# Fox attention with a bilinear feed-forward network: decay vectors spread over the partitions by GpSimd instead of by copying transfers

## The chip, the cores and the metric

The kernel runs on one core of a Trainium2 chip. The core has four engines that compute (TensorE, here PE with its weight loads as PEld; VectorE, DVE; ScalarE, ACT; GpSimd, POOL), a fifth, SyncE (SP), that mostly issues transfers, and 16 DMA engines. Each engine runs its own list of instructions in order and waits at semaphores for the others. The metric is the device time of one execution in microseconds (us); lower is better.

## What is computed

For 8 batches of 8 heads with 576 positions and head size 64, the reference forms attention scores with a decay, takes a causal softmax, and puts the result through a bilinear feed-forward network (d_model 512, d_ff 1536) on 4608 tokens:

```python
scores = scale * np.matmul(q, k.transpose(0, 1, 3, 2))
log_f = np.log(np.clip(f, 0.0001, 1.0))
cum = np.cumsum(log_f, axis=-1)
decay = cum[:, :, :, None] - cum[:, :, None, :]
scores = np.where(causal, -1000000000.0, scores + decay)
...
attn = attn / (np.sum(attn, axis=-1, keepdims=True) + 1e-09)
return np.matmul(attn, v)
...
x = attn_out.transpose(0, 2, 1, 3).reshape(B * S, H * D)
a = x @ w_a
b = x @ w_b
return a * b @ w_out
```

The part of the decay that varies along a row of scores is one vector of 576 numbers per head, the decay vector (`cum` of that head). In a tile of scores the 128 partitions are query positions, so each partition needs the same vector.

## The kernel before

Heads are worked in pairs: `t` from 0 to 31 is a pair, four pairs a batch, and two pairs (four heads, `u`) share their score matmuls. For each pair the kernel computes score tiles by 128 query rows (PE, line 390), then a row maximum, an exponential with its row sum (ACT, lines 537 and 543), a reciprocal (DVE, 550 and 552), a scaling by it (GpSimd, line 560, f16 in place), transposes of the probabilities (DMA transposes on SP's queue, line 576), the product with `v` (PE, lines 604 to 629) and a copy into `xT`. Once the tokens of a block are complete, the feed-forward network runs over them (PE, lines 877 and 897), with its copies and products on ACT and DVE and its stores on SP's queue (line 907). Matmuls of the network fill PE while the attention of later batches is on the other engines. After the last pair only the network's last blocks are left.

The first two batches (`DIRECT` = 2, pairs 0 to 7) add the decay with extra matmuls. The other 24 pairs take it from a tile `spread`: four buffers (`spread_79` to `spread_82`), each with the vectors of both heads of a pair on all 128 partitions. The cumulative sums are stored once in DRAM as `cum_d` (64 x 576). `load_spread` (line 451) reads two rows of it with one DMA that copies them to 128 partitions, 576 KB written. Then GpSimd makes masked copies (`mask_copy` 458, `mask_tail` 464, later `mask_last` 469), and DVE adds vector and scores and takes the maximum in one instruction (`do_decay`, line 508). A `spread` buffer is free for the pair four later once the last of these has read it.

GpSimd also casts q, k and v to f16 (lines 139 and 141).

The kernel is written as a list of small operations, and the table `ORDER` fixes the one sequence in which all of them are emitted; each engine's list is that sequence cut down to its own operations. `CHOICE` fixes the engine for those that can run on several. Nothing is reordered when it runs.

Of the kernel before, what the change touches and what calls it, by code (L numbers as in the profile page):

```python
# [9 lines left out]
FP32 = mybir.dt.float32  # L10
# [27 lines left out]
def kernel(  # L38
# [11 lines left out]
    nc = tc.nc  # L50
# [12 lines left out]
    def pool(name, bufs=1, **kw):  # L63
        return ctx.enter_context(tc.tile_pool(name=name, bufs=bufs, **kw))
# [7 lines left out]
    T = {}  # L72
# [27 lines left out]
    RING = {"S": 2, "bc": 4, "n32": 3, "n16": 2, "PA": 3, "PB": 2, "PTA": 2, "PTB": 2, "st": 6, "ht": 14, "a16": 3, "osb": 2, "ff": 4}  # L100
# [17 lines left out]
    osb_pool = pool("osb", RING["osb"])  # L118
    ps = pool("ps", 1, space=bass.MemoryType.PSUM)
# [177 lines left out]
    def batch_inputs(b):  # L297
# [4 lines left out]
        for which, part, gm in items:  # L302
# [18 lines left out]
            ld = op("S", "ldqk", lambda _, which=which, hh=hh: load_qk(b, which, hh))  # L321
# [13 lines left out]
            tp = op("D", "tqk", lambda _, which=which, hh=hh: transpose_qk(b, which, hh), cas)  # L335
# [304 lines left out]

    last_row = [[] for _ in range(RING["bc"])]
    ev_ops, late, last_pb = {}, {}, [[] for _ in range(RING["PB"])]

    def decay_rows(t):
# [17 lines left out]
        ld = op("S", "ldb", lambda _: load_spread(t), [o6])  # L662
# [306 lines left out]
    for n in [256, 256, 256, 384] + [512] * 6 + [384]:  # L969
# [13 lines left out]
        215 81 216 202 203 276 204 7 201 180 207 208 281 285 181-183 1641 90 1642 441 187 317 289 188 189  # L983
        318 290 166 323 324 295 297 296 190 1645 1643 1644 319 325 217 218 1646 1647 165 1648 88 229 192 231
        459 291 221 223 191 230 257 224 258 209 232 255 222 279 184 256 280 286 235-237 444 238 329 205 186
# [5 lines left out]
        1682-1684 1680 316 364 340 249 1685 283 251 443 379 252 376 20 250 1687 404 380 1688 1691 398 381  # L991
        449 344 407 546 1689 1690 409 452 382 408 1693 372 1692 1695-1697 365 1694 347 348 371 464 349 357
# [6 lines left out]
        523 483 1737 1740-1742 492 493 488 489 509 494 524 510 477 516 539 525 526 1738 527 470 451 462 497  # L999
        498 1743 495 466 428-430 499 431 547 484 437 439 438 440 490 530 531 500 457 491 537 501 1745 1746  # L1000
# [4 lines left out]
        553 551 606 636 566 573 1791 574 557 558 575 576 607-609 653 1790 1793 1794 1792 637 559 578 577 579  # L1005
        555 610 611 580 552 1795 1798 1799 650 615-617 582-584 581 1796 560 639 548 612 642 556 620 622 627
        654 600 544 614 618 1800 1803 1804 1807 621 585 613 587 619 629 623 624 586 626 1805 625 630 1801
        588-590 1806 591 593 592 628 1808 1811 657 1809 1813 1810 1812 669 1815 1817 702 703 739 704 651
        1816 643 1814 709 670 705 1819 1820 638 710 655 1818 711 1823 676 1821 1825 671 1822 640 712-714
# [4 lines left out]
        688 696 698 744 728 699 726 1857 1858 735 730 1854 1855 641 694 700 729 731 732 701 747 1861-1863  # L1014
# [5 lines left out]
        788-790 818 825 820 791 826 848 819 1892 821-823 1893-1895 855 900 1896 867 908 868 824 907 828 902  # L1020
# [3 lines left out]
        862 906 920 883 921 885 1916-1918 938 1919 886 1920 1921 888 889 922 923 1922 839 850 866 887 1924  # L1024
        893 894 935 942 890 895 854 926 844 891 896 892 927-929 897 924 933 1032 898 1923 1925 1926 1929 945
# [103 lines left out]
```

## Time and profile before

| | us |
|---|---|
| three runs, median (lowest to highest) | 405.43 (403.7 to 407.23) |
| the profiled execution: time | 402.69 |
| the profiled execution: span on the core | 400.9 |
| TensorE's mean granted clock | 0.985 |
| transfers of `spread` | 24 of 576 KB, median 5.9 from issue to landing |
| bytes moved in all | 80.71 MB, 201 GB/s over the span |

A profile row gives a source line, an engine, an operation and the tiles that it writes and reads, then a count, the busy time and the mean of one in nanoseconds, and the idle time of the engine just before such instructions with what ended it. Between the span and the device time lie 402.69 - 400.9 = 1.8 us that no row shows.

### The profile page before, as it was taken

To read this page: it belongs to the slowest core of one execution; us is meant where nothing else is said; L and a number is where in the kernel's file an instruction comes from. 1 tells how busy PE (TensorE), PEld (TensorE's weight loads), DVE (VectorE), ACT (ScalarE), POOL (GpSimd) and SP (SyncE) were. 2 spreads that over 40 slices of the span, in tenths; PEclk is the share of its full clock that TensorE was granted. 3 is DMA by queue.
4 is the path that set the end of the run, shared out by engine and by line. 5 is a ranking of instruction groups with operands and counts; after the bars stand their busy time and mean duration, and the time that the engine had idled before them with its cause. 6 is when DMAs were issued, how large, how long until landed. Compare 5 with 4: busy or idle time off the path is not lost.

```text
span 400.9 us, 10798 instructions
## 1 busy us (share of the span) xinstructions
PE 378.9 (95%) x3856; PEld 209.3 (52%) x3856; DVE 315.5 (79%) x958; ACT 250.6 (63%) x756; POOL 262.8 (66%) x438
## 2 busy tenths in 40 slices
PE   5679799989999999999999999999999999999996
PEld 5557575765846544444545454544454444444553
DVE  5879997979998988989899789899959893373450
ACT  2678895768768777758785777675868673310111
POOL 4988899787967796979696948697858753000000
PEclk9869999999999999999999999999999999999999
DMA  7999999999999999999899998999997827101102
GB/s 245 261 217 224 253 284 224 233 209 225 208 281 224 267 199 305 202 310 191 270 217 286 238 301 168 242 242 243 255 199 192 151 68 177 54 0 53 55 2 78
DMA packets 149466, 80.71 MB, mean 201 GB/s; under 512 B 130660, under 2 KB 133476, under 8 KB 149412
## 3 DMA queue, kind: packets, MB, share of 16 engines
q1 hardware_dynamic: 145492, 75.02, 79.1%
q0 software_dynamic: 3696, 4.72, 7.0%
q8 instruction: 30, 0.49, 0.5%
q10 hardware_dynamic: 224, 0.28, 0.2%
q14 instruction: 24, 0.20, 0.1%
HBM read 52.20 MB, written 9.58 MB: 154 GB/s over the span
## 4 chain that ended last, share of the span: by engine, by line
PE 69%; DMA 8%; DVE 8%; POOL 5%; ACT 4%; issue 4%; SPq 0%; POOLq 0%; ACTq 0%; DVEq 0%
PE psb L877 20%; PE psa L877 20%; PE pso L897 16%; PE sc L390 7%; DVE st L484 3%; PE pv L604 2%; DMA PTB<-PB 2%; POOL PA L560 2%; DMA spread<-cum_d 2%; DMA k<-in_k_dram 2%; PE idle L174 1%; DVE ht L888 1%; DVE S L508 1%; DMA out_dram<-osb 1%; DMA xT<-PA 1%
## 5 line engine op out<-in xcount | busy, mean ns | idle before, releaser
L877 PE MATMUL psb<-xT,wb 128*128 128x512 f16 (+2 forms) x528 | 115.2, 341 | 2.4 <-DVE a L141 1.3
L877 PE MATMUL psa<-xT,wa 128*128 128x512 f16 (+2 forms) x528 | 115.2, 341 | 0.5 <-ACT osb L137 0.2
L508 DVE CUSTOM_DVE_ANT_0 S<-sc,spread 128x128 f32<-128x128 f32 (+3 forms) x192 | 104.3, 567 | 7.8 <-PE sc L390 6.7
L560 POOL TENSOR_SCALAR PA<-PA,st 128x128 f16<-128x128 f16 (+2 forms) x180 | 84.4, 482 | 33.8 <-DVE st L552 19.8
L897 PE MATMUL pso<-wout,ht 128*128 128x512 f16 (+1 forms) x444 | 98.4, 374 | 0.0
L888 DVE TENSOR_TENSOR ht<-psb,a 128x512 f16<-128x512 f32 (+2 forms) x132 | 76.7, 588 | 14.1 <-PE psb L877 10.1
L543 ACT ACTIVATE PA<-S,st 128x256 f16<-128x256 f32 (+2 forms) x144 | 71.9, 501 | 22.9 <-DVE st L508 21.4
L877 PEld LDWEIGHTS <-wb 128*128 128x128 f16 x528 | 49.8, 98 | 45.7 <-issue 6.8
L877 PEld LDWEIGHTS <-wa 128*128 128x128 f16 x528 | 50.4, 98 | 42.7 <-issue 2.0
L560 POOL TENSOR_SCALAR PB<-PB,st 128x512 f16<-128x512 f16 (+1 forms) x90 | 62.8, 712 | 10.6 <-DVE st L552 5.9
L897 PEld LDWEIGHTS <-ht 128*128 128x128 f16 x444 | 41.8, 98 | 48.1 <-issue 2.8
L137 ACT CAST a<-psa 128x512 f16<-128x512 f32 (+2 forms) x85 | 42.7, 511 | 34.8 <-PE psa L877 33.4
L390 PE MATMUL sc<-kT,qT 32*128 32x128 f16 (+5 forms) x960 | 41.3, 272 | 6.8 <-DVE qT L294 4.6
L543 ACT ACTIVATE PB<-S,st 128x512 f16<-128x512 f32 x48 | 34.3, 716 | 8.1 <-DVE st L508 7.4
L484 DVE TENSOR_REDUCE st<-sc 128x1 f32<-128x576 f32 (+8 forms) x48 | 31.4, 693 | 6.8 <-PE sc L390 5.2
L141 DVE CAST a<-psa 128x512 f16<-128x512 f32 (+2 forms) x47 | 26.2, 558 | 11.3 <-PE psa L877 10.8
L390 PEld LDWEIGHTS <-qT 32*128 32x128 f16 (+1 forms) x960 | 19.0, 96 | 28.8 <-issue 12.3
L552 DVE RECIPROCAL st<-st 128x2 f32<-128x2 f32 x128 | 18.6, 157 | 11.5 <-ACT PB L543 6.1
L537 ACT ACTIVATE PB<-S,st 128x576 f16<-128x576 f32 x24 | 18.6, 775 | 13.9 <-DVE st L508 5.0
L543 ACT ACTIVATION_READ_ACCUMULATOR PA<-S,st 128x1 f32 x144 | 27.2, 189 | 0.0
L137 ACT COPY osb<-pso 128x512 f32<-128x512 f32 (+1 forms) x26 | 14.4, 563 | 20.3 <-PE pso L897 18.6
L141 POOL CAST k<-k 128x1152 f16<-128x1152 f32 (+2 forms) x16 | 22.1, 1384 | 5.0 <-DMA k<-in_k_dram 5.0
(87 smaller groups left out, 449.8 us busy)
## 6 DMA issues: line engine op xcount, KB each, us to landing
spread<-cum_d SPq DMA_DIRECT2D x24, 576.0 KB, 5.9
out_dram<-osb SPq DMA_DIRECT2D x35, 256.0 KB, 4.0
k<-in_k_dram SPq DMA_DIRECT2D x15, 576.0 KB, 6.5
q<-in_q_dram SPq DMA_DIRECT2D x15, 576.0 KB, 6.9
v<-in_v_dram SPq DMA_DIRECT2D x32, 256.0 KB, 6.7
wout<-in_moe_w_out_dram POOLq DMA_DIRECT2D x3, 512.0 KB, 11.0
wa<-in_moe_w_a_dram POOLq DMA_DIRECT2D x1, 1024.0 KB, 13.9
v<-in_v_dram SPq DMA_DIRECT2D x8, 128.0 KB, 6.0
```

What stands on the lines that cost most here:

```text
L137: nc.scalar.copy(out=out_, in_=in_)
L141: ENG[e].tensor_copy(out=out_, in_=in_)
L390: nc.tensor.matmul(out=dst, lhsT=lhsT, rhs=rhs, start=start, stop=stop, skip_group_check=True)
L484: nc.vector.tensor_reduce(out=m if i == 4 else st[:, 2 * i:2 * i + 2][:, h:h + 1] if isinstance(x, list) else m, in_=y, axis=AXX, op=MAX, ...
L508: nc.vector.tensor_tensor_reduce(out=o, in0=x, in1=y, scale=-1.0, scalar=3e38, op0=ADD, op1=MIN, accum_out=m)
L537: nc.scalar.activation(out=p_blocks(t, 4), in_=T[("s" if direct else "z", t, 4)], func=EXP, bias=st[:, 8:9], scale=sign, accum_out=st[:, 1 ...
L543: nc.scalar.activation(out=p_blocks(t, i)[:, :, h, :], in_=x.rearrange("p (j k) -> p j k", k=128), func=EXP, scale=sign, bias=st[:, c:c + ...
L552: nc.vector.reciprocal(out=st[:, 20 + 2 * i:22 + 2 * i], in_=st[:, 10 + 2 * i:12 + 2 * i])
L560: ENG[e].tensor_scalar(out=p, in0=p, scalar1=st[:, c:c + 1], scalar2=1.0, op0=MUL, op1=MUL)
L877: nc.tensor.matmul(out=p[:, 0:n], lhsT=w16[:, db, 128 * fb:128 * fb + 128], rhs=xTflat[db][:, t0:t0 + n], start=(db == 0), stop=(db == 3))
L888: nc.vector.tensor_tensor(out=ht[:, 0:n], in0=T.pop(("psb", t0, fb))[:, 0:n], in1=T.pop(("a16", t0, fb))[:, 0:n], op=MUL)
L897: nc.tensor.matmul(out=o, lhsT=T[("ht", t0, fb)][:, 128 * tb:128 * tb + 128], rhs=wout16[:, fb, c], start=(fb == 0), stop=(fb == 11))
```

## The change

The DMA that wrote two heads' vectors onto 128 partitions is gone. For four heads (`u`), one load brings four rows of `cum_d`, 9 KB, into a new tile `rw`, on partitions 0, 32, 64 and 96. For each pair, two GpSimd instructions (`partition_broadcast`) each copy one of these rows to all 128 partitions of `spread`. There are 12 loads and 48 broadcasts. `rw` has one buffer, and the ring `ht` (products of the network) has 13 buffers instead of 14. The masked copies are as before. `ORDER` and `CHOICE` are new throughout.

```diff
-    RING = {... "st": 6, "ht": 14, "a16": 3, "osb": 2, "ff": 4}
+    RING = {... "st": 6, "ht": 13, "a16": 3, "osb": 2, "ff": 4, "rw": 1}
...
-    def load_spread(t):
-        nc.sync.dma_start(out=spread[t % RING["bc"]][:, :, SM:SM + S],
-                          in_=cum_d.rearrange("(n h) s -> n (h s)", h=2)[t:t + 1, :].to_broadcast(
-                              [128, 2 * S]).rearrange("p (h s) -> p h s", h=2))
+    def load_rows(u):
+        x = T[("rw", u)] = rw_pool.tile([128, S], FP32, tag="rw", name="rw")
+        nc.sync.dma_start(out=x.rearrange("(h r) s -> h r s", r=32)[:, 0, :], in_=cum_d[4 * u:4 * u + 4, :])
+
+    def spread_rows(t):
+        for h in range(2):
+            nc.gpsimd.partition_broadcast(spread[t % RING["bc"]][:, h, SM:SM + S], T[("rw", t // 2)][RG[2 * (t % 2) + h], :])
...
-        ld = op("S", "ldb", lambda _: load_spread(t), [o6])
+        u = t // 2
+        if t % 2 == 0:
+            rw_ops[u] = op("S", "ldr", lambda _: load_rows(u), [o6])
+            rw_users[u] = take(rw_ops[u], "rw")
+        ld = op("P", "bcp", lambda _: spread_rows(t), [rw_ops[u]])
+        rw_users[u].append(ld)
...
     ORDER = """
-        42 44 43 61 0 1 59 46 52 62 63 45 47 48 15 35 64 66 49 67 26 3 68 31 53 54 38 10 22 2 70 65 25 14 50
...
```

The program has something that the diff does not show. Each GpSimd operation belongs to a library of instructions, and the built program holds a request to load a library wherever the next operation is not in the one loaded last. Such a request is a row `ISA` that names no tile; it has the line of the operation behind it. Before, there is one such request (library 0, ahead of the identity matrix). Now there are 43: that one, then 21 for library 1 ahead of broadcasts and 21 for library 0 ahead of the next `TENSOR_SCALAR` (20 at the scaling, one at a cast of q). Casts and masked copies run under either library.

GpSimd's list in the third batch, before, from the end of one group of pairs (the scalings of `PB`) to the start of the next (the scalings of `PA`). `spread_79` to `spread_82` are the four buffers of `spread`, and the 128x2x64 row is `mask_tail`:

```order
L560 TENSOR_SCALAR PB_77<-PB_77,st 128x576
L560 TENSOR_SCALAR PB_77<-PB_77,st 128x4x128 x2
L560 TENSOR_SCALAR PB_78<-PB_78,st 128x576
L560 TENSOR_SCALAR PB_78<-PB_78,st 128x4x128 x2
L464 AFFINE_SELECT spread_81<-spread_81 128x2x64
L141 CAST k_2391<-k_2113 128x1152
L141 CAST nv_74<-v_2273 64x512
L560 TENSOR_SCALAR PA<-PA,st 128x2x128
L139 TENSOR_SCALAR q_2495<-q_2061 128x1152
L560 TENSOR_SCALAR PA<-PA,st 128x2x128
```

The same place now, in the words of the changed kernel (lines are 1 to 4 higher; line 458 is the broadcast, and `L458 ISA` or `L564 ISA` without a tile is a request for a library):

```order
L140 TENSOR_SCALAR q_2428<-q_2209 128x1152
L468 AFFINE_SELECT spread_81<-spread_81 128x2x64
L458 ISA
L458 ISA spread_80<-rw 128x576 x2
L142 CAST nv_74<-v_2096 64x512
L564 ISA
L564 TENSOR_SCALAR PA<-PA,st 128x128
L458 ISA
L458 ISA spread_79<-rw 128x576 x2
L564 ISA
L564 TENSOR_SCALAR PA<-PA,st 128x128
L564 TENSOR_SCALAR PA<-PA,st 128x2x128 x2
```

Between the scalings of two groups now stand two pairs of broadcasts, with four requests for a library around them and one scaling between.

SP's queue at that place, before: loads of k, q and v, transposes of `PA` and `PB`, and two of the 576-KB loads of `spread`.

```order
L280 DMA q_2061<-in_q_dram 128x1152
L280 DMA k_2113<-in_k_dram 128x1152
L576 DMA_TRANSPOSE PTA<-PA 128x12x128
L264 DMA v_2273<-in_v_dram 64x8x64
L576 DMA_TRANSPOSE PTA<-PA 128x12x128
L576 DMA_TRANSPOSE PTB<-PB_77 128x13x128
L576 DMA_TRANSPOSE PTB<-PB_78 128x13x128
L452 DMA spread_79<-cum_d 128x2x576
```

SP's queue there now, where `rw` is the tile of four rows, and line 917 is a store of the output:

```order
L281 DMA q_2209<-in_q_dram 128x1152
L580 DMA_TRANSPOSE xT_70<-PA 128x6x128
L454 DMA rw<-cum_d 4x576
L281 DMA k_2329<-in_k_dram 128x1152
L580 DMA_TRANSPOSE PTA<-PA 128x12x128 x2
L580 DMA_TRANSPOSE PTB<-PB_77 128x13x128
L580 DMA_TRANSPOSE PTB<-PB_78 128x13x128
L265 DMA v_2479<-in_v_dram 128x8x64 x2
L917 DMA out_dram<-osb 128x512
L454 DMA rw<-cum_d 4x576
```

Each load of `rw` stands ahead of a load of k or q and of the next transposes, and with one buffer it can only go when both broadcasts that read the four rows before it are done.

More of the change, by code (lines that the diff above doesn't have):

```diff
@@ L99 @@
     SM = 3 * 128
-    RING = {"S": 2, "bc": 4, "n32": 3, "n16": 2, "PA": 3, "PB": 2, "PTA": 2, "PTB": 2, "st": 6, "ht": 14, "a16": 3, "osb": 2, "ff": 4}
+    RING = {"S": 2, "bc": 4, "n32": 3, "n16": 2, "PA": 3, "PB": 2, "PTA": 2, "PTB": 2, "st": 6, "ht": 13, "a16": 3, "osb": 2, "ff": 4, "rw": 1}
     PB = [fixed(f"PB{i}", [128, 13, 128]) for i in range(RING["PB"])]
@@ L118 @@
     osb_pool = pool("osb", RING["osb"])
+    rw_pool = pool("rwp", RING["rw"])
     ps = pool("ps", 1, space=bass.MemoryType.PSUM)
@@ L320, in batch_inputs @@
             hh = part
-            ld = op("S", "ldqk", lambda _, which=which, hh=hh: load_qk(b, which, hh))
+            ld = op("S", "ldqk", lambda _, which=which, hh=hh: load_qk(b, which, hh), size=TW)
             ld.after.extend(gate)
@@ L334, in batch_inputs @@
                 cas.append(ca)
-            tp = op("D", "tqk", lambda _, which=which, hh=hh: transpose_qk(b, which, hh), cas)
+            tp = op("D", "tqk", lambda _, which=which, hh=hh: transpose_qk(b, which, hh), cas, TW)
             nx.append(tp)
@@ L639, in do_ev4 @@
         cast(e, xT[pr][:, b, SF:S], T.pop(("pv4", t)))
+    rw_ops, rw_users = {}, {}
     last_row = [[] for _ in range(RING["bc"])]
@@ L1025 @@
-        893 894 935 942 890 895 854 926 844 891 896 892 927-929 897 924 933 1032 898 1923 1925 1926 1929 945
[10 rows of a table removed]
-        1985 1988 1071 1989 1992 1993 1225 1114 1086-1088 1084 1139 1119 1120 1085 1226 1136 1064 1116 1994
[5 rows of a table removed]
-        1145 1167 1236 1203 1160 1192 1150 1146 1233 2019 1205 1172 2022 2021 1244 1153 1168 1171 1206-1209
[3 rows of a table removed]
-        2042-2044 2046 1186 1213 1220 1296 1303 1249 2048 1272 1264 1222 2047 1298 2045 1305 2049 1219 1224
-        2050-2052 1266 1297 1304 1273 2055 1252 1237 1238 2053 1253 1299 1333 1234 1256 1259 1257 1232 1255
@@ L1048 @@
-        1337 1260 1235 1267 1274 1276 1300 1306-1308 1310 1311 1241 1313 1277 1279 1301 1278 2056 2057 2060
-        1334 1280 2058 2054 1312 1314 1258 1261 1284 1285 2061 2062 1286 1302 1317 1269 1318 1309 1239 1316
-        1423 1315 2065 1281 2066 1338 2059 1254 1246 1331 1268 1319 1242 1250 1426 2063 1275 1320 1282 1262
-        1322 1283 2067 1287 1321 2070 2071 2074 1324 1329 1323 1325 1289 1326 1290-1292 2072 1328 2068 1341
-        1293 1335 1386 2076 1327 1388 1353 1294 1393 1395 2075 2078 1339 2073 1354 1387 1361 1295 2077 1332
@@ L1053 @@
-        1360 1288 1427 1330 1445 2080 1441 1240 2079 1429 1389 2081 1428 1355 1394 1356 1390 2082 2084 1396
-        1357 1362 1363 2083 2085-2087 2090 2091 2088 1346 2092 1364 1342 1359 1345 2089 1424 1391 1349 1365
-        1446 1343 2093 1344 2064 1358 2069 1350 1400 1401 1431 1402 1367 1403 2094 2096 2095 2098-2100 1368
[13 rows of a table removed]
-        1601 2172 1556 1600 1602-1604 1623 1549 2173 1567 2174 2175 1546 1605 1568 1606 1538 2178 1572 1569
-        1557 2176 1564 1573 1534 2177 2179 1607 1574-1576 2180 1550 1577 1579 1578 2181 1608 2182-2185 1580
@@ L1071 @@
-        1581 2132 1571 1570 1617 2186 2187 1609 2188 2191-2193 2196 1583 1582 1610 1612 2197 1618 1611 2198
-        2201 2202 1613 1614 1616 2194 1615 1624 2195 2189 1620 1621 2190 2199 1626 1627 2203 2204 2206 2205
-        1619 1625 1622 2208 1628 2200 2207 2209 2210 2212 2211 2214 2213 2216 2215 2217 2218 2220 2219 2222
-        2224 2223 2221 2225 2226 2228 2227 2230 2232 2229 2231 2234 2233 2236 2235 2237-2246 2248 2247 2250
-        2252 2249 2251 2253-2261 2264-2266 2262 2263 2269 2267 2270-2272 2274 2275 2278 2276 2273 2280 2277
@@ L1076 @@
-        2268 2279 2281 2282 2284 2283 2285-2287 2290 2291 2288 2289 2292 2294 2295 2293 2296-2300 2302-2304
-        2301 2305-2310 2312 2311 2314 2313 2316 2315 2318 2320 2319 2317 2322 2323 2321 2324 2327-2329
-        2332-2334 2337 2338 2325 2326 2330 2331 2339-2341 2335 2336
+        0 15 1 42 44 59 25 21 43 6 32 2 39 61 45-47 52 53 60 26 62 63 16 35 10 24 48-51 28 40 33 54 4 64-66
+        30 67 68 55 70 31 71 72 22 74 14 78 69 91 73 85 267 5 104 92 34 75-77 84 12 19 11 105 93 79 36 7 98
@@ new lines @@
+        94 27 17 110 8 95 106 99 56 112 111 82 100 96 80 38 97 107 116 117 123 101 109 119 57 118 108 103
+        102 113 129 135 125 114 124 115 131 86 268 141 120 148 126 211 225 136 212 128 130 219 226 137 270
+        138 150 83 127 233 132 133 142 220 13 139 234 149 121 151 154 144 143 155-157 167 161 122 58 162 152
[3 rows of a table added]
+        181 187 182 183 285 274 289 317 188 189 1653-1655 90 201 209 323 290 1656 295 275 165 197 178 221
[6 rows of a table added]
+        265 346 367-369 395-397 445 401 1690 1691 1694 316 1695 1696 373-375 403 402 354 442 355 446 1692
[9 rows of a table added]
@@ new lines @@
+        1754 496 1757 1758 433 528 498-500 510 1755 651 511 1761 531 1762 501 532 1763 1759 502 548 1760 551
[3 rows of a table added]
+        608 1751 572 1789 1791 602 1790 1793 567 1794 1792 573 568 574 634 1795 1797-1799 552 556 555 559
+        1796 1801 560 601 569 1803 610 611 1802 657 577 578 1805 1806 561 613 1800 612 557 1804 654 575 553
+        580 614 742 579 616-618 1807 576 644 558 615 1810 1811 641 584 585 550 1756 631 653 581 619 562 583
+        620 1812 635 586 622 623 546 554 1808 1809 624 625 589 626 590 582 629 587 621 640 627 1813 591 1815
@@ new lines @@
+        1816 1819 1817 1818 1820 1821 660 672 679 592 593 1823 1824 1822 628 1827 632 588 594 595 705 630
+        642 645 1825 673 674 747 749 712 706 675 1826 676 1829 681 1828 1830-1833 707 713 715 1834 1835 1837
[4 rows of a table added]
+        696 700 701 731 732 697 745 702 1864 1865 1868 835 703 751 796 1866 733-735 704 737 1869 1870 798
[5 rows of a table added]
+        816 750 788 839 1904 795 822 823 841 794 824 829 825 1908 1905 860 831 830 821 858 1910 826-828 905
+        907 906 908 912 832 1909 1036 1912 872 947 949 948 880 873 1911 1913 1914 1916 1915 1918 874 943 914
@@ new lines @@
+        913 875-877 1917 915 1919 1922 1923 916 879 918 1920 882 861 878 865 1921 862 840 881 1924 909 911
+        945 917 846 842 883 1051 864 868 1872 1037 1925 869 866 1877 867 919-922 886 887 923 1926 889 1927
+        870 924 885 926 888 1928 1931-1933 884 893 863 910 925 894 927 944 890 1929 855 891 928 871 1934 895
+        892 847 859 1936-1938 898-900 849 850 896 931 901 902 1941 1930 932 1942 1943 933 929 843 897 934
+        935 1033 940 951 904 903 1038 996 1003 930 937 1935 936 938 939 1946 1947 1939 963 1944 941 848 1052
@@ new lines @@
+        1948 970 965 964 1039 997 972 998 971 1034 1950 999 1951 1949 973-975 1000 1004 966 1954 1952 1955
[5 rows of a table added]
+        1050 1107 1106 1079 1979 1112 1982 1983 1981 1984 1042 1045 1985-1987 1108 1990 1991 1074 1081 1988
[6 rows of a table added]
+        2018 1205 2020 1164 2017 2019 2022 2024 2023 1252 1253 1172 1166 1206 1171 2021 1141 2025-2027 2030
[13 rows of a table added]
+        2094 2096 2095 2097-2099 2102 2103 1248 2100 1356 1366 1339 2101 1367 1357 1438 1369 1456 1345 1352
[13 rows of a table added]
+        1605 2173 2176 2175 2177-2179 1607 2180 1450 1552 1556 1573 1602 1553 1574 1559 2181 1555 1554 1560
[3 rows of a table added]
@@ new lines @@
+        1624 1593 2198 2199 2197 1623 1625 1588 1595 1626 2200 2203-2205 2208 1594 1630 1628 2209 2210 2213
+        2214 1627 2201 1636 2202 2206 2207 1632 1633 2211 1638 2215 1639 2218 2216 2220 1637 1640 1631 1634
+        2212 2219 2222 2223 2221 2224-2226 2228 2227 2229 2230 2232 2231 2234 2233 2235 2238 2236 2237 2240
+        2239 2241-2243 2246 2244 2245 2248 2247 2249 2250 2252 2251 2254 2253 2255-2260 2262 2263 2266 2264
+        2261 2265 2267 2217 2268 2271 2272 2269 2270 2273 2276-2278 2281 2274 2275 2279 2280 2282-2286 2288
@@ L1079 @@
+        2287 2290 2289 2292 2291 2294-2296 2293 2297 2298 2300 2299 2302 2303 2301 2304 2306 2305 2308 2307
+        2310 2309 2312 2311 2314 2315 2313 2316-2318 2320 2319 2322 2323 2326 2321 2324 2327 2325 2328-2341
+        2344 2342 2343 2345 2346 2349 2347 2350 2351 2348 2352 2353
     """
     CHOICE = """
-        SAPDPPPPPAAPPPPPADADDDADADDAAADAAADADDAADDAAAADADAAADAAADAAAAAAAAAAAAADAAAAADAAAADDADDAADAADADAAAAA
-        AAADAAADDDDDADDADAADADDDAADAADAAAAAAAAADDAAADDADAAAAAADAAAAAADDAAAAADAAAADAAADDADAAAAAAADDDADAAAAAA
@@ L1083 @@
-        AAAADAADDADAAAADDAAAAAAAAAAAAAADADDDAAAADAAAAADDDAADDADDDAADDDADDADADDAAAAAAS
+        SADDPPDAAAAPAPADDDAAADDDADAAAADDAAAAADDDDDADADDADAAADDADADAADAAAADDDAAAAAAAADAADADAAADDDDAADAAAAAAA
+        DADDAADADDDAADAADADDAAAAAADAADAAAADAAADAADADAAADAADDAAAAAAAADAAAAAAAAAAAAAADADADAAAAAAADAADAAAAAAAA
+        AAAAAAAADAAADAAADAAAAAADADAAAAADADDAAAADDAAAADAAADADDDADDADAADAAADDDAAAAADSAA
     """
```

15 lines of the change are left out of this document (removed), and 135 rows, old and new, of the table ORDER.

## Prediction

> **What bounds the kernel now.** I read the page's head first, then each engine's busy time in long stretches (columns: PE, PEld, DVE, ACT, POOL, then PE's granted clock, DMA share and GB/s).
>
> ```profile
> span 400.9 us, 10798 instructions
> PE 378.9 (95%) x3856; PEld 209.3 (52%) x3856; DVE 315.5 (79%) x958; ACT 250.6 (63%) x756; POOL 262.8 (66%) x438
> ...
> 0.00:40.00 40.00, 28.72 (x480) 24.12 (x484) 30.84 (x77) 25.27 (x75) 30.54 (x56) 0.87 0.99 237
> 40.00:100.00 60.00, 53.99 (x860) 37.96 (x858) 52.33 (x147) 45.69 (x149) 51.09 (x82) 1.00 1.09 238
> 100.00:336.00 236.00, 235.00 (x2168) 115.77 (x2168) 207.28 (x694) 169.32 (x513) 181.19 (x302) 1.00 0.98 226
> 336.00:380.00 44.00, 44.00 (x255) 21.33 (x253) 18.39 (x30) 7.06 (x14) 0.00 (x0) 1.00 0.20 61
> ```
>
> TensorE is the bound: from 100 to 380 us it is busy for 235.0 + 44.0 of 280.0 us at full granted clock. What it loses lies early: 40 - 28.72 = 11.3 us before 40, and 60 - 53.99 = 6.0 us between 40 and 100. A change that only relieves the DMA engines can win some of that, and nothing later. GpSimd works until 336. From 40, just ahead of the first decay vector in use, to 336 it is busy for 51.09 + 181.19 = 232.3 of 296 us, so it has 63.7 us to spare. Behind its last instruction lie 402.7 - 336 = 66.7 us of network matmuls, in which it has no part. So what is put on GpSimd is free up to about 60 us, and beyond that it delays the scalings, their transposes, the products with v and in the end the last blocks of the network.
>
> Next, GpSimd's groups (busy, mean ns, then idle before with its releaser), and the waits for `spread`:
>
> ```profile
> L560 POOL TENSOR_SCALAR PA<-PA,st 128x128 f16<-128x128 f16 (+2 forms) x180 | 84.4, 482 | 33.8 <-DVE st L552 19.8 <-issue 7.9 <-ACT PA L543 3.7
> L141 POOL CAST k<-k 128x1152 f16<-128x1152 f32 (+2 forms) x16 | 22.1, 1384 | 5.0 <-DMA k<-in_k_dram 5.0
> L458 POOL TENSOR_SCALAR_AFFINE_SELECT spread<-spread 128x768 f32<-128x768 f32 x24 | 20.8, 867 | 3.3 <-DMA spread<-cum_d 3.3
> ...
> L464 POOL TENSOR_SCALAR_AFFINE_SELECT spread<-spread 128x128 f32<-128x128 f32 x24 | 6.9, 295 | 10.1 <-DMA spread<-cum_d 10.1
> ```
>
> The old loads cost GpSimd 3.3 + 10.1 = 13.4 us of waiting. These are inside the 63.7 us of idle time, on an engine that is not the bound, and PE's waits do not show them.
>
> **The change, part by part.** First, what it removes, by the issue rows (KB each, median us to landing):
>
> ```profile
> spread<-cum_d SPq DMA_DIRECT2D x24, 576.0 KB, 5.9
> ...
> v<-in_v_dram SPq DMA_DIRECT2D x8, 128.0 KB, 6.0
> ...
> cum_f<-in_f_dram ACTq DMA_DIRECT2D x1, 144.0 KB, 2.7
> ```
>
> 24 x 576 KB = 14.2 MB of the 80.71 MB moved go; 12 x 9 KB come back, 0.1 MB. The DMA share of 0.98 to 1.09 until 336 says that the transfers queue for each other, and so the transposes should land sooner. What that can be worth is read from the chain of waits (start us, length, what), at its two longest transfers between 40 and 100:
>
> ```profile
> 71.08 7.30 DMA PTB<-PB
> ...
> 80.03 4.50 DMA xT<-PA
> ```
>
> By the 4.2 us that is the median for these 28 transposes of `PB`, the first of them is stretched by 3.1 us.
>
> ```profile
> PTB<-PB SPq DMA_TRANSPOSE x28, 4.2
> ```
>
> So this part is worth between nothing and the 6.0 us that PE is idle there. I take 0 in the forecast, since the part below decides.
>
> Second, the 48 broadcasts. No row shows one. From below: a masked copy of 768 f32 elements takes 867 ns, so 576 take 0.65 us, and 48 of them 31 us. From above: moving data between partitions, as DVE's transposes do, with 576 f32 elements a partition:
>
> ```profile
> L294 DVE STREAM_TRANSPOSE kT<-k 128x576 f32<-128x576 f32 x16 | 19.5, 1218 | 1.0 <-POOL k L141 0.9
> ```
>
> I take these 1.22 us, since a broadcast also crosses partitions: 48 x 1.22 = 58.6 us. Even this alone would about fit into the 63.7 us.
>
> Third, the requests for a library, 42 more than before. One stands in the trace, between setting up `ident` and masking it (start, us, what):
>
> ```profile
> 2.23 0.21 POOL masks.py:197 MEMSET ident<- 128x128 f16 x1
> 2.52 0.29 POOL masks.py:199 TENSOR_SCALAR_AFFINE_SELECT ident<-ident 128x128 f16<-128x128 f16 x1
> ```
>
> Between the end at 2.44 and the start at 2.52 lie 0.08 us. That is the lowest bound; but it asks for library 0 at the start, ahead of any other, and need not have loaded anything. The only change of an engine's tables that the trace shows is ACT's:
>
> ```profile
> L201 ACT ACT_TABLE_LOAD x2 | 2.6, 1283 | 1.3 <-PEq L1113 1.3
> ```
>
> 1.28 us each. If a change of library fetches code from DRAM, it takes what a small load takes: 2.7 us for 144 KB at the empty start, 6.0 us for 128 KB among the other transfers. I take a fetch, because code for an engine that works as a set of programs has to come from somewhere, and the middle of 2.7 and 6.0, 4.35 us: 42 x 4.35 = 182.7 us. All requests stand in GpSimd's own list, and what is behind one waits: casts of k, q and v, masked copies, and the scalings, for which the transposes on SP's queue wait.
>
> The Trainium skill (GPSIMD Engine Reference, section 2.1, Instruction dispatch) says that the first call after a kernel library was loaded pays about 6 us, measured as 5.95, with no instruction of its own in the profile. By that the sum below would hold 42 x 5.95 = 249.9 instead of 182.7, and come to 648 us. The one row here, 0.08 us, does not show it.
>
> Sum: GpSimd needs 232.3 + 58.6 + 182.7 = 473.6 us where 296 are there, with every idle moment filled. The attention ends 473.6 - 296 = 177.6 us later, and PE, whose list has the same work behind it, cannot fill that: 402.7 + 177.6 = 580 us. This stands on the profiled execution, 402.7, which is 2.7 us below the median of the runs, 405.4; against this spread of the sum that difference is nothing.
>
> Fourth, the wait of the broadcast for its load. The 9 KB land within 6.0 us, the row for 128 KB, and the load is issued ahead of the broadcast by whole groups of scalings; I cost it at nothing. If that cover is gone, 12 x 6.0 = 72 us at most, when GpSimd is not already late. SP's queue can be held too: the one `rw` buffer keeps a load until the broadcasts before it have run, and behind it stand loads of k and q and the transposes. When GpSimd is late this delays what GpSimd itself would do later, and is already in the sum.
>
> Fifth, the new order. At the start the first cast of k is split between GpSimd and DVE. It was two instructions on GpSimd on the chain:
>
> ```profile
> 7.83 2.54 POOL k L141 x2
> ```
>
> At most half, 1.3 us, can go, and as much could come back in the moved casts of q; zero. One buffer of `ht` less is covered by PE's 1.0 us of idle time between 100 and 336 being so small that these buffers hardly ever stop it; zero, or a few times 1 us if they begin to.
>
> **The rivals.**
> (a) Only the way into library 1 pays, and library 0 stays loaded. For it: the request for library 0 in the trace cost 0.08 us. Against it: that one changed nothing. 21 x 4.35 = 91.4; 232.3 + 58.6 + 91.4 - 296 = 86.3; 489 us.
> (b) A change of library costs what ACT's table load costs. For it: the nearest kind of row. Against: tables of one engine are not code for many programs. 42 x 1.28 = 53.9; 344.8 - 296 = 48.8; 451 us.
> (c) Libraries are resident and a request is free, 42 x 0.08 = 3.4 us, and the DMA engines' relief decides. This one ends faster: GpSimd needs 232.3 + 31.2 + 3.4 = 266.9 of 296 us, the transposes no longer queue behind 576-KB loads, and of the 6.0 us of PE's idle time between 40 and 100 all goes: 396.7 us; with the 3.1 us of the one stretched transpose, 399.6. It decides from the point where broadcasts and requests together stay under about 60 us.
> (d) As (c), but the broadcasts at 1.22 us fill GpSimd: 232.3 + 58.6 + 3.4 = 294.3 of 296 us. Its waits for reciprocals (19.8 us at the scalings of PA) can then no longer be had beside the work; with up to half of them added, 402.7 to 413 us.
>
> **How the numbers follow.** The forecast, both ways pay a fetch: 0.42, between 42 x 2.7 with broadcasts of 0.65 (232.3 + 31.2 + 113.4 - 296 = 80.9; 484 us) and 42 x 6.0 with 1.22 (232.3 + 58.6 + 252 - 296 = 246.9; 650 us). (a) 0.16, (b) 0.13, (c) 0.15, (d) 0.14. The likeliest gives 580. The range reaches to 650, the forecast's own end, and down to 398, which takes in (a), (b), (d) and the lower half of (c)'s gain; about 0.15 is outside, its own tails among it. One per cent, 4 us, is what a measurement of this kernel tells from no change, the three runs lying 3.5 us apart. Faster by more than that: most of (c), 0.13. Within it: the rest of (c) and half of (d), 0.09. Slower: the forecast, (a), (b) and half of (d), 0.78.
>
> **What would show it.** Right: gaps of some us on GpSimd, with no instruction in them, ahead of each broadcast and of the next scaling; GpSimd's last scaling at about 510 us instead of 336; PE idle through the attention, waiting for products whose transposes wait for GpSimd; the DMA share far below 0.98. Gaps only ahead of broadcasts would be (a). Broadcast rows of 0.65 to 1.22 us would show the second term. Wrong: broadcasts that start within 0.1 us of the instruction before them, with PE still busy from 100 to 380; then (c) or (d) holds, and a shorter transpose of `PB` near 71 us would tell them apart.

## The result, and the profile after

The changed kernel takes 676.25 us (median of four runs, 675.56 to 676.66) against 404.56 us before: 1.671 times as long, 95% interval 1.665 to 1.677. The profiled execution took 675.56 us.

The page's head after, then engines in three long stretches (columns: PE, PEld, DVE, ACT, POOL, PE's granted clock, DMA share, GB/s):

```profile
span 673.6 us, 10897 instructions
PE 424.5 (63%) x3856; PEld 226.0 (34%) x3856; DVE 314.8 (47%) x958; ACT 257.3 (38%) x763; POOL 294.3 (44%) x479
...
0.00:40.00 40.00, 30.29 (x496) 25.77 (x497) 32.78 (x81) 28.20 (x82) 24.14 (x47) 0.87 1.00 240
40.00:609.00 569.00, 332.87 (x3002) 168.72 (x3002) 257.50 (x839) 217.23 (x659) 270.15 (x432) 0.78 0.43 94
609.00:674.00 65.00, 61.37 (x360) 31.47 (x357) 24.48 (x40) 11.82 (x23) 0.00 (x0) 0.99 0.16 53
```

No engine looks like a bound now. PE, which hardly stopped between 100 and 380 us before, is busy 58.5% of the long stretch, and GpSimd, which sets the pace, shows only 270.15 of 569 us. The missing time is in the column of idle time. GpSimd's groups over the whole execution (busy, mean ns, then idle before with its releasers):

```profile
L564 POOL TENSOR_SCALAR PA<-PA,st 128x128 f16<-128x128 f16 (+2 forms) x180 | 83.0, 470 | 151.4 <-issue 144.9 <-DVE st L556 6.4
L564 POOL TENSOR_SCALAR PB<-PB,st 128x512 f16<-128x512 f16 (+1 forms) x90 | 62.1, 701 | 11.9 <-issue 9.3 <-DVE st L556 2.3
L458 POOL PARTITION_BROADCAST spread<-rw x48 | 38.4, 862 | 131.9 <-issue 93.7 <-DVE st L556 12.4 <-DVE st L512 7.3
...
L140 POOL TENSOR_SCALAR q<-q 128x1152 f16<-128x1152 f32 x14 | 19.5, 1392 | 8.7 <-issue 7.7 <-DVE st L556 1.0
```

"issue" is idle time in which the engine waited for nothing that the profile shows. It stands ahead of exactly the instructions that need a library: 131.9 us ahead of broadcasts, and 144.9 + 9.3 + 7.7 = 161.9 us ahead of scalings and the cast of q. One of these 161.9 is no library load, 3.3 us ahead of a scaling late in the kernel where no request stands, which leaves 158.6. Together that is 290.5 us for 42 loads, 6.9 us each. Where other releasers are named ahead of a broadcast, it is the same gap: all 21 gaps ahead of broadcasts take 5.8 to 7.6 us, and the 21 on the way back 7.0 to 9.4. The timeline of GpSimd in one place (start, length, what, idle before) shows how it reads:

```profile
158.24 0.28 POOL L468 TENSOR_SCALAR_AFFINE_SELECT spread<-spread 128x128 f32<-128x128 f32 x1
164.54 1.61 POOL L458 PARTITION_BROADCAST spread<-rw  x2 [6.01 <-DMA v<-in_v_dram]
165.98 0.67 POOL L142 CAST nv<-v 64x512 f16<-64x512 f32 x1
173.72 0.36 POOL L564 TENSOR_SCALAR PA<-PA,st 128x128 f16<-128x128 f16 x1 [7.07 <-issue]
179.97 1.60 POOL L458 PARTITION_BROADCAST spread<-rw  x2 [5.89 <-issue]
189.97 1.28 POOL L564 TENSOR_SCALAR PA<-PA,st 128x128 f16<-128x128 f16 x3 [8.40 <-issue]
...
607.16 1.36 POOL L564 TENSOR_SCALAR PB<-PB,st 128x512 f16<-128x512 f16 x2 [1.09 <-DVE st L556]
```

About 6 us into library 1 ahead of a broadcast of two rows, some 7 to 8 us back ahead of the next scaling, with a cast that needs no library in between. The broadcasts themselves are cheap, 1.6 us for two. GpSimd's last scaling, the last line, ends at 608.5 us. Everyone else waits for that engine, DVE directly and PE behind it, as their waits show (engine, line, waited for: us in total, times, longest):

```profile
DVE S L512 <- POOL spread L473: 130.3, 14, 25.5
...
PE sc L391 <- DVE st L512: 73.5, 16, 19.4
```

The transfers did get lighter, 66.66 MB in place of 80.71 MB and a DMA share of 0.43 in the long stretch. Loads of k land in 4.3 us at the median where they took 6.5. That gains nothing while GpSimd sets the pace.

### The profile page after: what moved, and what is told of

The parts are those of the page before. It is cut to its first block, busy times and chain, and to the rows that moved or that the text cites. A ratio compares the mean times of both kernels' runs of the same rounds, so it can differ in the third digit from the quotient of the medians.

```text
span 673.6 us, 10897 instructions
## 1 busy us (share of the span) xinstructions
PE 424.5 (63%) x3856; PEld 226.0 (34%) x3856; DVE 314.8 (47%) x958; ACT 257.3 (38%) x763; POOL 294.3 (44%) x479
## 2 busy tenths in 40 slices
DMA packets 143034, 66.66 MB, mean 99 GB/s; under 512 B 130324, under 2 KB 133140, under 8 KB 142980
## 5 line engine op out<-in xcount | busy, mean ns | idle before, releaser
L887 PE MATMUL psb<-xT,wb 128*128 128x512 f16 (+2 forms) x528 | 127.3, 368 | 61.6 <-ACT osb L138 31.6
L564 POOL TENSOR_SCALAR PA<-PA,st 128x128 f16<-128x128 f16 (+2 forms) x180 | 83.0, 470 | 151.4 <-issue 144.9
L887 PE MATMUL psa<-xT,wa 128*128 128x512 f16 (+2 forms) x528 | 128.7, 371 | 16.3 <-ACT a L138 16.3
L391 PE MATMUL sc<-kT,qT 32*128 32x128 f16 (+5 forms) x960 | 51.2, 307 | 102.6 <-DVE st L512 73.5
L907 PE MATMUL pso<-wout,ht 128*128 128x512 f16 (+1 forms) x444 | 103.7, 389 | 0.0
L458 POOL PARTITION_BROADCAST spread<-rw x48 | 38.4, 862 | 131.9 <-issue 93.7
L138 ACT CAST a<-psa 128x512 f16<-128x512 f32 (+2 forms) x100 | 50.6, 512 | 57.1 <-PE psa L887 53.5
L564 POOL TENSOR_SCALAR PB<-PB,st 128x512 f16<-128x512 f16 (+1 forms) x90 | 62.1, 701 | 11.9 <-issue 9.3
L391 PEld LDWEIGHTS <-qT 32*128 32x128 f16 (+1 forms) x960 | 22.8, 107 | 130.3 <-issue 83.4
L295 DVE STREAM_TRANSPOSE kT<-k 128x576 f32<-128x576 f32 x16 | 19.4, 1212 | 31.1 <-POOL k L142 30.7
L608 PE MATMUL pv<-PTA,nv 128*64 128x384 f16 (+1 forms) x144 | 16.1, 294 | 15.9 <-DVE ht L898 15.9
L138 ACT CAST xT<-pv 128x512 f16<-128x512 f32 (+2 forms) x33 | 15.1, 469 | 27.1 <-PE pv L620 13.8
```

What stands on the lines that cost most here:

```text
L138: nc.scalar.copy(out=out_, in_=in_)
L295: nc.vector.transpose(out=y.rearrange("p (a s w) -> p w a s", a=2, s=NSLOT), in_=x.rearrange("p (w a d) -> p w a d", a=2, d=32))
L391: nc.tensor.matmul(out=dst, lhsT=lhsT, rhs=rhs, start=start, stop=stop, skip_group_check=True)
L458: nc.gpsimd.partition_broadcast(spread[t % RING["bc"]][:, h, SM:SM + S], T[("rw", t // 2)][RG[2 * (t % 2) + h], :])
L564: ENG[e].tensor_scalar(out=p, in0=p, scalar1=st[:, c:c + 1], scalar2=1.0, op0=MUL, op1=MUL)
L887: nc.tensor.matmul(out=p[:, 0:n], lhsT=w16[:, db, 128 * fb:128 * fb + 128], rhs=xTflat[db][:, t0:t0 + n], start=(db == 0), stop=(db == 3))
```

## The experiments

The theory: library loads hold GpSimd, some 6 to 7 us each, and everything else in the change is small. Against it stood that the new order, the broadcasts themselves, or the wait for the rows and SP's queue behind them cost the time. Ten programs ran; the times of those that compute the attention are compared with the kernel before on the same chip.

**The new order with the old transfers.**

```diff
     def load_rows(u):
...
+        pass
...
     def spread_rows(t):
-        for h in range(2):
-            nc.gpsimd.partition_broadcast(...)
+        nc.sync.dma_start(out=spread[t % RING["bc"]][:, :, SM:SM + S],
+                          in_=cum_d...[t:t + 1, :].to_broadcast([128, 2 * S])...)
```

> The new order with the old 576-KB copying transfers at the places of the broadcasts, and no load of rows. Theory (the library loads are the cost): no GpSimd gap of 5 us or more is left, so the time is that of before within 3%, 395 to 417 us. Rival (the new order itself, written for another timing, is the cost): over 450 us.

Measured 422.98 us, 1.046 (1.042 to 1.051): above the 417 us at which the expected range ended, and far below the rival's 450 us. No gap put down to issue reaches 5 us. So the 1.67 is gone with the broadcasts, but 4.6% stays. GpSimd waits for these transfers ahead of its masked copies:

```profile
L462 POOL TENSOR_SCALAR_AFFINE_SELECT spread<-spread 128x768 f32<-128x768 f32 x24 | 20.8, 867 | 31.7 <-DMA spread<-cum_d 31.7
...
L468 POOL TENSOR_SCALAR_AFFINE_SELECT spread<-spread 128x128 f32<-128x128 f32 x24 | 7.1, 296 | 19.8 <-DMA spread<-cum_d 19.8
```

These are 51.5 us where the kernel before has 13.4. A transfer of 6 us now stands where a broadcast of 1.6 us was meant to, which would explain the rest. To test it, each transfer was emitted right behind the last use of its buffer:

```diff
+    def sooner(seq):
+        # each copying transfer right behind the last use of its buffer
...
+            i = max([seq.index(o) for o in [*held.get(tag, []), o6]])
+            if i < seq.index(x):
+                seq.remove(x)
+                seq.insert(i + 1, x)
```

> As e1_copy_in_new_order, but each copying transfer is emitted right behind the last use of its buffer, not where the broadcast stood. If the 4.6% of e1 came from transfers of 6 us that were issued just ahead of the masked copies (GpSimd waited 51 us for them, 13 us in the kernel before), the time falls to 400 to 410 us. If the order itself is the worse one for a kernel with copying transfers, it stays at 418 us or more.

Measured 460.75 us, 1.144 (1.135 to 1.152). That is outside the 400 to 410 us of the first theory. The 418 us or more of the second hold by the number, but the run does not bear that theory out either, because the edit made a new wait: SP's queue works in order, and the transfers that wait for their buffer now stand ahead of DMA transposes and loads that could go. SP's own waits name it:

```profile
SPq L456 <- DVE st L512: 53.4, 13, 12.0
```

This run says nothing on where the 4.6% come from; that stays argued. For the question here it is enough that order and transfers together cost 4.6%; the copies without a library, below, test the order with the new loads.

**Library loads without the rest of the change.** The kernel before, unchanged but for one tiny broadcast ahead of each first masked copy:

```diff
...
     def mask_copy(t):
+        nc.gpsimd.partition_broadcast(word[:, 8:16], word[RG[0], 0:8])
         c = spread[t % RING["bc"]]
```

> The kernel before, with all its transfers and its order, and one broadcast of 8 words to a tile that nothing reads ahead of each of the 24 first masked copies; this asks for 48 library loads. Theory: 48 loads of 5.8 and 7.3 us (medians read in the changed kernel) are 314 us, 24 small broadcasts some 7 us, less about 50 us of idle time that they fill: 404 + 271 = 675 us, between 640 and 710. Rival (the broadcasts of 576 words, or their wait for the rows, are the cost): the time stays under 430 us.

Measured 716.33 us, 1.771 (1.759 to 1.782), a little over the expected 640 to 710. The gaps ahead of these broadcasts, the 24 ways into library 1, are 148.9 us:

```profile
L459 POOL PARTITION_BROADCAST word<-word x24 | 6.8, 282 | 148.9 <-issue 136.4 <-DVE ht L891 12.5
```

Old order, old transfers, no row loaded, 8 words instead of 576, and the kernel is slower still than the changed one, with 48 loads instead of 42. The added 313.5 us are 6.5 us a load; I had reckoned that GpSimd's idle time would hide about 50 us of it, and less of it was hidden. (The expectation's 5.8 us for the way in was a little low, too: the median of these gaps in the changed kernel is 6.0 us.)

**The change without library loads.** The new order and its 9-KB loads, with plain copies of the same shape in place of broadcasts:

```diff
...
-            nc.gpsimd.partition_broadcast(spread[t % RING["bc"]][:, h, SM:SM + S], T[("rw", t // 2)][RG[2 * (t % 2) + h], :])
+            nc.gpsimd.tensor_copy(out=spread[t % RING["bc"]][:, h, SM:SM + S], in_=T[("rw", t // 2)])
```

> The changed kernel with its order and its 9-KB loads, but GpSimd copies a tile of zeros and four rows onto itself, partition by partition, in place of each broadcast (576 f32, under either library), so that the decay vectors are wrong on most partitions. No library is changed. Theory: GpSimd has 48 x 0.7 = 34 us more work, inside its 63.7 us of idle time, and PE stays the bound: 397 to 413 us. It shows what the change would be worth were libraries free. Rival (the wait for the rows, or SP's queue behind the one row buffer, costs too): over 420 us.

Measured 401.26 us, 0.994 (0.990 to 0.998).

```profile
L459 POOL COPY spread<-rw 128x576 f32<-128x576 f32 x48 | 30.6, 667 | 0.0
```

With 30.6 us more work on GpSimd, the new order, the loads of rows and one `rw` buffer, the kernel is as fast as before, or 0.6% faster. So neither the order nor the rows nor SP's queue costs anything here, and with libraries free the change would have been worth about 0.6%, as far as these copies stand for broadcasts, which take 38.4 us in all.

**The transfers alone.**

```diff
     def load_spread(t):
+        if t >= 2 * NP + RING["bc"]:
+            return
```

> The kernel before with the copying transfers of the first four pairs only; the other 20 pairs use what lies in the buffers, so their decay is wrong. 11.8 MB of transfers are gone and nothing is added. Theory: PE is the bound from 100 us on, so at most the 6.0 us that it is idle between 40 and 100 us can go: 397 to 405 us. Rival (the transfers hold the kernel back all along): under 392 us.

Measured 403.29 us, 0.9995 (0.996 to 1.003). Between 100 and 336 us the DMA share falls to 0.81, and PE has 234.91 us busy of 236 as before:

```profile
100.00:336.00 236.00, 234.91 (x2175) 116.31 (x2174) 208.72 (x702) 170.97 (x519) 180.69 (x302) 1.00 0.81 177
```

So the 20 transfers that were taken away, which all lay behind 100 us, cost this kernel nothing that can be measured. The four that stayed are those of the stretch between 40 and 100 us, so on that stretch this run says nothing, against what its expectation had in mind. The copies without a library have none of the 24, and there PE is busy 56.44 of these 60 us instead of 53.99,

```profile
40.00:100.00 60.00, 56.44 (x885) 39.86 (x883) 53.83 (x162) 46.93 (x156) 56.67 (x91) 1.00 1.05 204
```

and this 2.5 us is about the 0.6% by which that kernel is faster. But it is hardly more than what separates two executions with the same work there: in the run with the four transfers left, which up to 100 us is the kernel before, PE is busy 51.87 us.

```profile
40.00:100.00 60.00, 51.87 (x841) 36.53 (x831) 50.01 (x139) 43.69 (x142) 49.81 (x80) 1.00 1.13 232
```

So where the 0.6% come from, and how much of it is the transfers and how much the new order, is not shown.

**Fewer loads.** The changed kernel with both pairs' broadcasts of four heads together, 24 loads instead of 42:

```diff
+    def together(seq):
+        # the broadcasts of two pairs one behind the other, at the later place
...
+            for o in late:
+                seq.remove(o)
+            j = seq.index(y)
+            seq[j + 1:j + 1] = late[1:]
+            seq.insert(j, x)
```

> The changed kernel with both pairs' broadcasts of four heads one behind the other, at the later of the two places, and their masked copies behind them; 24 library loads in place of 42. Theory: 18 loads of 6.8 us go, 676 - 122 = 554 us, between 535 and 575. Rival (loads are hidden in part, or something else of the change costs): over 600 us.

Measured 566.87 us, 1.403 (1.396 to 1.411), inside the expected range: 109.4 us less than the changed kernel for 18 loads, 6.1 us each. The time goes with the number of loads.

**The load by itself.** A program of GpSimd instructions, first with the DMA engines idle, then beside a queue of 576-KB transfers. No part of the reference is computed.

```diff
+        for _ in range(6):
+            spread_(S)
+            scale()
...
+        for n in range(72):
+            nc.sync.dma_start(out=load[n % 4]..., in_=cum...)
+        for _ in range(8):
+            spread_(S)
+            scale()
```

> No part of the reference is computed: GpSimd alternates a broadcast (library 1) and a scaling of 128x512 f16 (library 0), first with nothing else running, then behind a VectorE chain of some 10 to 20 us, then beside a queue of 576-KB transfers. The cost of a library load by itself. Theory: 5.6 us into library 1 and 7.0 us back with nothing else running (the shortest gaps of the changed kernel); beside transfers up to 2 us longer, as a fetch by the DMA engines would be; and hidden where the instruction behind it has to wait for VectorE anyway (it then starts within 0.2 us of VectorE's end). Rival (a load is work of GpSimd alone): the same length beside transfers. Rival on hiding (the load starts only when the instruction behind it may run): 5 to 7 us after VectorE's end. Broadcasts of 8 and 1152 words give its slope: 0.86 us at 576.

GpSimd's timeline, one round trip alone and three beside the transfers:

```profile
90.23 0.86 POOL L73 PARTITION_BROADCAST dst<-src  x1 [5.97 <-issue]
98.34 0.68 POOL L70 TENSOR_SCALAR p<-p,s 128x512 f16<-128x512 f16 x1 [7.25 <-issue]
...
239.78 0.86 POOL L73 PARTITION_BROADCAST dst<-src  x1 [10.58 <-issue]
252.13 0.68 POOL L70 TENSOR_SCALAR p<-p,s 128x512 f16<-128x512 f16 x1 [11.49 <-issue]
262.07 0.86 POOL L73 PARTITION_BROADCAST dst<-src  x1 [9.26 <-issue]
273.48 0.68 POOL L70 TENSOR_SCALAR p<-p,s 128x512 f16<-128x512 f16 x1 [10.55 <-issue]
283.70 0.87 POOL L73 PARTITION_BROADCAST dst<-src  x1 [9.54 <-issue]
294.59 0.68 POOL L70 TENSOR_SCALAR p<-p,s 128x512 f16<-128x512 f16 x1 [10.02 <-issue]
...
330.28 0.68 POOL L70 TENSOR_SCALAR p<-p,s 128x512 f16<-128x512 f16 x1 [7.50 <-issue]
337.09 0.86 POOL L73 PARTITION_BROADCAST dst<-src  x1 [6.12 <-issue]
```

and the DMA share in these three stretches (columns here: DVE, POOL, granted clock, DMA share, GB/s):

```profile
0.00:206.00 206.00, 69.74 (x38) 32.64 (x43) 1.00 0.00 1
206.00:316.00 110.00, 0.00 (x0) 8.34 (x13) 1.00 0.98 386
316.00:361.00 45.00, 0.00 (x0) 4.70 (x7) 1.00 0.02 6
```

Alone, about 6 us into library 1 and 7 us back. Beside full DMA engines, 9.3 to 10.6 and 9.8 to 11.5 us, more than the 2 us that I had allowed for, and 6.1 and 7.5 us again when the transfers are through. So a load is not work of GpSimd alone. It fits a fetch that shares the way with the transfers, but the fetch itself is not in the records, so that stays argued. The chain on VectorE in this program was done each time before GpSimd came to the instruction that needs it, so it tested nothing about hiding. A second program did:

```diff
...
+            spread_(8)
+            nc.scalar.copy(out=busy[:, 0:8], in_=dst[:, 0:8])
+            for _ in range(3):
+                nc.scalar.copy(out=busy, in_=busy)
+            nc.scalar.copy(out=gate, in_=busy[:, 0:512])
+            scale(gate)
...
```

> No part of the reference is computed: GpSimd alternates small broadcasts and scalings, and the one behind each library load needs the result of a chain of ScalarE copies of over 10 us that starts when the instruction before the load ends. Theory (a load needs nothing from the instruction behind it, so idle time of GpSimd covers it, as the sum of the prediction had it): that instruction starts within 0.3 us of ScalarE's end. Rival: 5.6 us (into library 1) or 7.1 us (back) after it.

```profile
20.59 0.62 ACT L90 CAST gate<-busy 128x512 f16<-128x512 f32 x1
21.32 0.69 POOL L70 TENSOR_SCALAR gate<-gate,s 128x512 f16<-128x512 f16 x1 [12.16 <-ACT gate L90]
...
33.60 1.15 ACT L95 COPY gate<-busy 128x1152 f32<-128x1152 f32 x1
34.98 0.28 POOL L73 PARTITION_BROADCAST dst<-gate  x1 [12.96 <-ACT gate L95]
```

The scaling starts 21.32 - 21.21 = 0.11 us after ScalarE's end, the broadcast 34.98 - 34.75 = 0.23 us. A load is done beneath such a wait of 12 to 13 us, with idle DMA engines: it needs nothing from the instruction behind it.

**GpSimd's time alone.** Copies as long as the loads, and no load:

```diff
...
+    def fill():
+        for _ in range(10):
+            nc.gpsimd.tensor_copy(out=rw, in_=rw)
...
+        fill()
         for h in range(2):
             nc.gpsimd.tensor_copy(out=spread[t % RING["bc"]][:, h, SM:SM + S], in_=T[("rw", t // 2)])
+        fill()
```

> As e3_copies_no_library (copies in place of broadcasts, decay vectors wrong), with 10 more GpSimd copies of 128x576 f32 in place ahead of, and 10 behind, 21 of the 24 pairs of copies: 42 x 10 x 0.667 = 280 us of GpSimd time, about what the 42 library loads held it for (285 us), at nearly the same places, and no load. Theory (a load costs by the time in which GpSimd does nothing else, and in no other way): 660 to 690 us, as the changed kernel. Rival (loads also slow the transfers or the other engines): clearly below it, under 640 us.

Measured 681.39 us, 1.684 (1.664 to 1.705).

```profile
L461 POOL COPY rw<-rw 128x576 f32<-128x576 f32 x420 | 280.1, 667 | 24.5
```

280.1 us of useless copies do what the loads did. They come with 24.5 us of idle time of their own, in gaps of under 1 us, so that they hold GpSimd some 14 us longer than the 290.5 us of the loads; the copies in place of the broadcasts are 7.8 us shorter, and the kernel takes 5.1 us more than the changed one. A library load costs by the time in which GpSimd can do nothing else; nothing more is needed to explain the result.

**GpSimd without library 0.** From the first broadcast on, the scalings go to VectorE and ScalarE and the casts of q to ScalarE, so that one load is left behind the start:

```diff
+        if which == "q" and "spread yet" in T:
+            e = "A"
...
-        ENG[e].tensor_scalar(out=p, in0=p, scalar1=st[:, c:c + 1], scalar2=1.0, op0=MUL, op1=MUL)
+        if "spread yet" not in T:
+            ENG[e].tensor_scalar(out=p, in0=p, scalar1=st[:, c:c + 1], scalar2=1.0, op0=MUL, op1=MUL)
+        elif i < 3:
+            nc.vector.tensor_scalar(out=p, in0=p, scalar1=st[:, c:c + 1], scalar2=1.0, op0=MUL, op1=MUL)
+        else:
+            nc.scalar.activation(out=p, in_=p, func=COPY, scale=st[:, c:c + 1])
```

> The changed kernel, but from the first broadcast on GpSimd does no operation of library 0: the scalings of PA run on VectorE, those of PB and the casts of q on ScalarE. The broadcasts stay, one library load stays. Theory: without 41 loads the time falls to that of PE plus what VectorE lacks: it is busy 207 of 236 us between 100 and 336, and 144 scalings of 0.1 to 0.5 us (no row shows one) come to it; 400 to 450 us. Rival (the broadcasts or their rows cost by themselves): over 500 us.

Measured 495.08 us, 1.226 (1.220 to 1.232): 181 us faster than the changed kernel, and still outside the 400 to 450 us that I expected. The scalings are work that their new engines did not have before:

```profile
L572 ACT ACTIVATE PB<-PB,st 128x512 f16<-128x512 f16 (+1 forms) x87 | 59.7, 732 | 2.4 <-DVE st L559 1.6 <-DVE st L557 0.8
L570 DVE TENSOR_SCALAR PA<-PA,st 128x128 f16<-128x128 f16 (+2 forms) x168 | 59.0, 377 | 1.0
```

59.0 us more for DVE, which was busy 207 of 236 us in the attention, and 59.7 us for ACT, on lists written for another division. Of the chain that ended last, DVE now has 27%, ACT 26% and GpSimd 2%, though between 100 and 336 us neither of the two is full (192.84 and 177.14 of 236 us). The run mixes two effects and does not tell how much of the 181 us the loads alone are worth.

This run shows one more load, at a place where no other has it, ahead of the masking of `ident`:

```profile
9.84 0.28 POOL masks.py:199 TENSOR_SCALAR_AFFINE_SELECT ident<-ident 128x128 f16<-128x128 f16 x1 [8.91 <-issue]
```

The request for library 0 stands there in all versions of the kernel, and in the others the gap is at most 0.3 us. This version is the only one whose last operation bound to a library is a broadcast. So the library seems to stay from one execution to the next, and a request to be free where its library is there already; this is inferred from the one run.

No version that ran beats the kernel before by more than the 0.6% of the copies without a library, which are not a broadcast. To keep that speed with rows spread by GpSimd would take a broadcast and a scaling in one library; it was not tried.

## Why the prediction was wrong

The mechanism was right and a size was off: 580 us was forecast, 676 measured, beyond the 650 at which the range ended. The signs came: gaps ahead of the broadcasts and of the next scalings, PE idle for 236 of the 569 us from 40 us on, a DMA share of 0.43, and GpSimd's last scaling at 608.5 us where about 510 was named.

- **The price of a library load**, the third part of the sum, is the step that failed. It was put at 4.35 us, the middle between a load of 144 KB at the empty start (2.7) and one of 128 KB among other transfers (6.0): 182.7 us for 42. Measured 290.5 us, 6.9 each. Both rows were transfers of data, and a load of a library with nothing else running already takes about 6 us in and 7 us back. Beside a full DMA it takes up to 11.5. So 4.35 us was too low even for idle DMA engines, the upper row was no upper bound, and the end of the range built on it fell short. That end had even been helped by broadcasts priced 20.2 us too high. That a load is a fetch, the reason given for the choice, fits its growing beside transfers and is otherwise not shown. The 0.08 us taken as the lowest bound were, by the run without library 0, most likely a request whose library was there already.
- The sentence on the Trainium skill (GPSIMD Engine Reference, section 2.1, Instruction dispatch) came nearer: 5.95 us a load, by which the estimate was 648 us. The runs agree with it for the way into library 1 with idle DMA engines (5.6 to 6.4 us in the program of loads alone). The way back costs about 1 us more, and the page's figure does not hold beside transfers.
- **The broadcasts** were put at 48 x 1.22 = 58.6 us; they take 38.4 us, 0.86 us each and 0.80 back to back. The lower row (0.65 us, a masked copy) was the nearer one.
- **GpSimd's other work and the tail** held. It had 232.3 us of other work from 40 us on, and has 270.15 - 38.4 = 231.8. Behind its last scaling, which ends at 608.5, lie 675.6 - 608.5 = 67.1 us where 66.7 was taken.
- **Idle time filled to the last**: nearly. From 40 to 608.5 lie 568.5 us; less 270.15 busy and 290.5 of loads, 7.9 us were left where 0 was assumed. The sum with measured sizes: 580 + (290.5 - 182.7) - (58.6 - 38.4) + 7.9 = 675.5 us.
- **The wait for the 9-KB load, the one `rw` buffer, the new order, one `ht` buffer less**, costed at nothing: shown together by the copies without a library, 0.994.
- **The removed transfers**, costed at 0 of at most 6.0 us: nothing behind 100 us, and between 40 and 100 at most the 2.5 us that PE gained in the copies without a library, which is hardly more than the 2.1 us between two executions with the same work there.
- The rivals: (a), a load in one direction only, fell, for both directions pay. (b), 1.28 us as for ACT's table, fell. (c) and (d) needed free libraries; with libraries left out the time is 0.6% under before, between no change and (c), which had 0.8 to 1.5%.

## What to carry to other kernels

Look in the built program for requests to load a library when an operation of another kind comes to GpSimd, and count them: here the price of the 48 new instructions was 38 us and that of the 42 loads around them 290 us, and the source shows none of these. In the trace each load has two rows `MODIFY_POOL_CONFIG` of at most 0.13 us on GpSimd's queue, 84 here, and then the gap. If a kernel must mix libraries, group the work under each, or put a load where GpSimd waits for another engine for longer than the load takes: waits of 12 to 13 us hid it wholly with idle DMA engines. And first take the suspected cost away: one run without 20 of the 24 transfers showed that there was nothing to win by removing those.

## What the runs showed of the hardware

The time of a load of a GpSimd library is not a constant: about 6 us into library 1 and 7 us back with idle DMA engines, 9 to 11.5 us at a DMA share of 0.98. GpSimd's profile shows it as idle time put down to "issue", or to another engine that had long been done.

A GpSimd instruction can be stretched by VectorE. In the program of loads alone, VectorE ran scalings of 128x4096 f32 from 11.6 to some 42 us, and the same broadcast and the same scaling took up to 3.25 and 2.57 us instead of 0.86 and 0.68; five more instructions that ran into such scalings took 0.4 to 1.4 us longer than alone. The two longest:

```profile
11.32 3.25 POOL L73 PARTITION_BROADCAST dst<-src  x1 [5.58 <-issue]
22.16 2.57 POOL L70 TENSOR_SCALAR p<-p,s 128x512 f16<-128x512 f16 x1 [7.58 <-issue]
```

TensorE's granted clock was low where it waited: 0.78 in the long stretch of the changed kernel, where PE is busy 332.87 of 569 us, and 0.99 in the last 65 us, where it is busy 61.37. The useless copies, which hold the others up as the loads do but load nothing, gave 0.77 in their long stretch, so the low clock does not come from the loads themselves.
